# Staging buffers of the weight conversion: pairs and w_out tiles in turn, spare columns and a third buffer

## The chip, the cores and the metric

The kernel runs on one core of a Trainium2 chip. The metric is the device time of one execution in microseconds; three runs of the kernel before took 836.95, 836.95 and 829.41 us. TensorE is called PE in the rows, ScalarE is ACT, VectorE is DVE, SyncE is SP, GpSimd is POOL.

## The reference

Attention with a local or strided mask over 4 batches, 8 heads, 576 positions and 64 dimensions gives x (2304 tokens x 512). Two feed-forward layers follow:

```python
def _moe_ref(x, w_in, w_out, s, b):      # 512 -> 2048 -> 512
    h = x @ w_in
    r = np.maximum(h, 0.0)
    g = s * (r * r) + b
    return (g @ w_out).astype(np.float32)

def _moe2_ref(x, w_in, w_out):           # the same shapes
    h = x @ w_in
    g = h * np.cos(h)
    return (g @ w_out).astype(np.float32)
```

All inputs are float32, and so is the result.

## The kernel before, in words

Every float32 operand of a matmul is split into a high and a low half of a shorter kind, and a product is three matmuls: high x high, high x low, low x high. The weights arrive as 64-bit words (the host only views the float arrays so) and must be turned into float32 and split on the chip, on ScalarE and VectorE; this is the conversion that the change touches.

**Stages.** First the attention runs, with the first slots of layer one between its steps. A slot (40 of them, index t) is one 128-wide part of the hidden layer for a block of tokens: four groups of matmuls into `h_ps`, the activation, and later four groups into `acc` (line 942). The slots cover eight of the sixteen hidden parts of layer one for all tokens. The other eight, and all of layer two's first product, go through units (loop over `u`): a unit is one pair of hidden parts for one region of 768 tokens, seven products of six matmuls each (line 1996, Strassen-like, on sums and differences of operands), with the activation behind it. Units 0 to 11 belong to layer one (three regions, pairs 4 to 7, the order turned in the middle region), units 12 to 19 to layer two's first region. The second product of each unit comes two units later as "triples": eight per unit of layer one (line 1886, each three matmuls of 512 and three of 256 columns), twelve of 512 columns per unit of layer two (line 1876). Two products' PSUM banks alternate; ScalarE evacuates P1, P6 and P7 into `q` (line 2008), VectorE adds the other banks to it and writes `h` (line 1976), ScalarE starts the activation on `h` (line 1433), `gh` and `gl` are its halves. After unit 19 the rest of layer two runs in blocks, with an order written out by hand.

**The conversion jobs.** `jobs2` lists jobs: for each pair of layer one's last four and of layer two's eight, first two pair jobs (`pair_ops`, m = 0, 1: a piece of w_in, converted into `ta`, four sums in `ts`, then halves in the tiles `ob` and `oa`), then two w_out jobs (`out_ops`: one tile, converted into `tw`, or for layer two's even tiles into the spare columns of the `q0` tile, `rq`, and then split into `ow`). The halves are stored to DRAM (`wfa`, `wfb`, `wfc`, `w2s`; for layer two the converted tile itself too, `w2f`) and loaded again as operands (`wfl`, line 1279; `w2l`, line 1312) when a buffer comes free. At the end come six jobs for sums of w_out tiles. Once layer two begins (`late` is set, unit 12), the halves go to other places.

`ob`, `oa` and `ow` are all tiles of one pool tag, `v`, with two buffers that alternate in the order of allocation; an allocation waits until the stores from the tile that it replaces have landed. A job is a generator; each step yields one instruction or an empty step. After attention a pair job has 4 + 4 + 6 + 3 = 17 steps (two of the first four empty), a w_out job 4 + 5 = 9 (two of the first four empty, one later, and for layer one the place of the `w2f` store as well). The load for the job after next is issued in the middle of a job.

**What sets the order.** `bg2_step(n)` adds n to a budget and issues one step for each whole unit of it. It is called eight times per slot from slot 15 on with a rate of `BG2`, and in a unit once after each of the seven products and after each triple (fifteen places in a unit of layer one) with the rate `BG2_UNIT[u]`. All is then placed by a scheduler in each engine's own queue; an instruction may be put ahead of others that were written before it when it is thought to be ready. `tc.issue_after(ins)` orders what is issued within it behind `ins` on the engine of `ins`; it adds no instruction. Before, only the first step of a job is put behind the last relu. SP's queue issues nearly all DMAs in order: raw loads, stores and the loads `wfl` and `w2l`.

The buffers of `w2l` are six tiles with the tags w10 to w15. `BUFS` and `w2_load` say which tile goes where and in which order; a buffer whose last triple is done takes its next tile at once (`load_w2`). Buffer w13 holds layer one's tile of pair 4 until the triples of unit 8, which are issued in unit 10, and then layer two's second tile, needed by the triples of unit 12, which are issued in unit 14.

Of the kernel before, what the change touches and what calls it, by code (L numbers as in the profile page):

```python
# [107 lines left out]
]  # L108
LAST_USE = {"P2": 0, "P5": 1, "P3": 2, "P4": 3}
UNIT0 = ["P1", "P2", "t", "P6", "P5", "P7", "P3", "P4"]  # L110
UNIT = ["P1", "P2", "P6", "P5", "P7", "t", "P3", "P4"]
BG2 = ((15, 1.2), (18, 2.2), (22, 1.0), (30, 1.6), (36, 0.6), (38, 1.2))
BG2_UNIT = (1.2, 2.0, 2.0, 1.4, 1.4, 1.5, 1.5, 1.4, 1.6, 1.7, 1.7, 1.7, 1.4, 1.4, 1.4, 1.4, 1.4, 1.4, 1.4, 1.4, 1.6, 1.6)
NSUM = 6
# [17 lines left out]
def net(ctx, tc, qkl, qks, rqk, vloc, vstr, rv, wi1, wo1, wp1, wo2, wp2, s, b, out):  # L132
# [56 lines left out]
    def to_f32(t, raw):  # L189
        tu = t.bitcast(U32)  # L190
        if raw.shifted:
            top = top_halves()
            t16, mid = raw.halves, raw.middles
            if len(t.shape) == 3:
                top, t16, mid = (x.rearrange("p (i c) -> p i c", i=t.shape[1]) for x in (top, t16, mid))
            out16 = consts.bitcast(F16)[:, 1::2]
            if len(t.shape) == 3:
                out16 = out16.rearrange("p (i c) -> p i c", i=t.shape[1])
            return [
                lambda: nc.scalar.activation(out16, t16, AF.Copy, scale=0.5),  # L200
                lambda: nc.vector.scalar_tensor_tensor(
                    tu, mid, 13, top.bitcast(U32), ALU.logical_shift_right, ALU.bitwise_or
                ),
                lambda: None,
                lambda: None,
            ]
# [176 lines left out]

    late = {}

    def begin_layer2():
# [19 lines left out]
    def pair_ops(raw, ly, p, m):  # L406

        ta = conv_tile("ta").rearrange("p (i c) -> p i c", i=4)
        yield from to_f32(ta, raw)
# [4 lines left out]
        for d, x, y, op in ((s1, a21, a22, ALU.add), (s2, s1, a11, ALU.subtract), (s3, a11, a21, ALU.subtract), (s4, a12, s2, ALU.subtract)):  # L414
            yield lambda d=d, x=x, y=y, op=op: nc.vector.tensor_tensor(d, x, y, op)
        apart = bool(late)
        if apart:
            obs = late_out(0)
# [18 lines left out]
        if apart:  # L437
# [3 lines left out]
            for h in range(2):  # L441
# [4 lines left out]

                yield store
        else:
            yield lambda: nc.sync.dma_start(out=wb[:, :, m, :], in_=ob.bitcast(F32).rearrange("p x h c -> p x (h c)"))
            yield lambda: nc.sync.dma_start(out=wa[:, m, :], in_=oa.bitcast(F32)[:, :512])  # L450
            yield lambda: nc.sync.dma_start(out=wc[:, m, :], in_=oa.bitcast(F32)[:, 512:])
        stored2.add(("pair", ly, p, m))

    def out_load(ly, n):
        return Raw(raw_tile("oraw"), wo_raw[ly][n])

    def out_ops(raw, ly, n):
        t = whole = q0_tile()[:, HT:] if ly and n % 2 == 0 else conv_tile("tw")
        yield from to_f32(t, raw)
        bg2_load()  # L460
        if late:
            os = late_out(n % 2)
            t = t.rearrange("p (x c) -> p x c", x=2)
        else:
            o = io_p.tile([P, 2, 512], F32R, tag="v", name="ow")
            os = [o[:, h, :] for h in range(2)]
        apart = bool(late)
        k = raw.scale
        assert raw.shifted or not ly
        yield lambda: split_hi(os[0], t, k)  # L470
        yield lambda: nc.sync.dma_start(out=w2f[n // 2][:, n % 2, :], in_=whole) if ly else None
# [17 lines left out]
    def sum_ops(raw, p):  # L489

        assert late
        c = raw.rearrange("p (f c) -> p f c", f=2)
        t13, t24 = (conv_tile(x).rearrange("p (x c) -> p x c", x=2) for x in ("t13", "t24"))
# [3 lines left out]
        bg2_load()  # L497
        pair = [(t13, late_out(0)), (t24, late_out(1))]
        for t, o in pair:
            yield lambda t=t, o=o: split_hi(o[0], t, 256.0)  # L500
        for t, o in pair:
            yield lambda t=t, o=o: split_lo(o[1], t, o[0], 256.0)
        for x, (_, o) in enumerate(pair):
# [6 lines left out]

            yield store
        stored2.add(("sum", p))

    jobs2 = []
# [18 lines left out]
    def bg2_load():  # L533
        if jobs2 and len(loaded2) < (1 if gp else 2):
            load, ops, args = jobs2.pop(0)
            loaded2.append(ops(load(*args), *args))

    def bg2_step(n):
        due2[0] += n
        while due2[0] >= 1:  # L540
            due2[0] -= 1
            if now2[0] is None:
# [397 lines left out]

    def mm(*args, **kw):
        nc.tensor.matmul(*args, **kw)  # L942

# [317 lines left out]

    def have(key):
        while key not in stored2:
            bg2_step(1)

    wft, w2t = {}, {}
# [15 lines left out]
    BUFS = [2, 3, 4, 5, 0, 1]  # L1282
    NSTAY = 2
    w2_load = {b_: [] for b_ in BUFS}
    w2_key, w2_last = {}, {}
# [572 lines left out]
    def triple():  # L1858
# [11 lines left out]
        gh, gl = g2[key]  # L1870
        w = w2t[n]
        start = opens[a] and f == 0
        stop = closes[a] and f == 1
# [74 lines left out]
    for u in range(NU2 + 2):  # L1948
# [29 lines left out]
        for what in UNIT0 if u == 0 else UNIT:  # L1978
            if what == "t":
                if u == NU1:  # L1980
                    fetch(2)
                triples(u)
                continue
            x, fi, j, bi, st = PRODUCTS[what]
            while (ly, s_, j) not in formed:
                bg2_step(1)
                tick()
# [4 lines left out]
            fo, lo = P * fi, 256 if x < 3 else P  # L1992
            for m in range(2):
                wh, wl = w[:, m, fo : fo + P], w[:, m, lo + fo : lo + fo + P]
# [135 lines left out]
```

## Time and profile before

| what | value |
|---|---|
| three runs | 836.95, 836.95, 829.41 us; median 836.95 |
| profiled execution | 829.91 us, span 828.1 us |
| TensorE busy | 815.9 us (99%) |
| weight loads busy | 732.4 us (88%) |
| VectorE busy | 629.4 us (76%) |
| ScalarE busy | 586.5 us (71%) |
| granted TensorE clock, mean | 1.000 |

The span runs from the first to the last instruction. Busy time is the union of an engine's instructions; weight loads overlap matmuls. In stretches of the span, the attention and the first slots lie before 145 us, the conversions beside slots until 271, layer one's units until about 480, layer two's first region until 600, the blocks after it.

### The profile page before, as it was taken

The page shows a single profiled execution, that of the slowest core. Times are in us where ns is not written, and L with a number is a line of the kernel's source. Part 1 is how long each engine was busy: PE and PEld are TensorE (multiplying, and loading weights), DVE is VectorE, ACT ScalarE, POOL GpSimd, SP SyncE. Part 2 cuts the span into 40 slices and gives each one's busy share as a digit, 9 for nine tenths or more (in the row PEclk, how much of TensorE's full clock was granted, in tenths as well). Part 3 has the DMA queues.
Part 4 walks back from the last instruction along what each step waited for, and adds up shares of the span by engine and source line. Part 5 has one row for each costly group of instructions (what it writes and reads, how often), then busy time and mean ns, then how long its engine had stood idle before and what let it go on. Part 6 is the DMA issues. An engine that isn't in the chain of part 4 may idle for free.

```text
span 828.1 us, 15377 instructions
## 1 busy us (share of the span) xinstructions
PE 815.9 (99%) x5545; PEld 732.4 (88%) x5545; DVE 629.4 (76%) x1183; ACT 586.5 (71%) x1232; POOL 20.1 (2%) x74
## 2 busy tenths in 40 slices
PE   8899999999999999999989999999999999999998
PEld 5677888788988898999989999888899999999998
DVE  6898555776868769965856598777758999578985
ACT  6897667668876887777768567557568765589753
POOL 3120000000000000000000000000000000000000
PEclk9999999999999999999999999999999999999999
DMA  9775232376889998796799989899797878874675
GB/s 334 240 249 165 82 104 97 127 261 225 325 318 365 359 351 271 284 366 215 283 334 338 305 286 365 297 315 383 257 350 262 273 252 258 286 254 153 207 250 179
DMA packets 101980, 219.98 MB, mean 266 GB/s; under 512 B 9104, under 2 KB 53392, under 8 KB 101904
## 3 DMA queue, kind: packets, MB, share of 16 engines
q1 hardware_dynamic: 100176, 211.82, 74.3%
q10 hardware_dynamic: 1728, 7.18, 2.3%
q8 instruction: 44, 0.72, 0.3%
q14 instruction: 32, 0.26, 0.1%
HBM read 163.91 MB, written 55.05 MB: 264 GB/s over the span
## 4 chain that ended last, share of the span: by engine, by line
PE 76%; ACT 8%; DVE 7%; DMA 7%; issue 1%; POOL 0%; SPq 0%; ACTq 0%; POOLq 0%; DVEq 0%
PE acc L942 10%; PE h_ps L942 10%; PE acc L1876 8%; PE pa L1996 8%; PE acc L1695 8%; PE pb L1996 8%; PE acc L1886 7%; PE acc L1565 6%; PE pa L1565 3%; PE pb L1565 3%; ACT part L684 2%; DVE graw L1157 2%; DVE xlo L171 2%; DMA wfc<-oa 2%; DMA w2s<-ow 2%; DMA wfb<-ob 1%
## 5 line engine op out<-in xcount | busy, mean ns | idle before, releaser
L942 PE MATMUL h_ps<-xhi,w 128*128 128x512 f32 (+1 forms) x320 | 102.4, 378 | 0.6 <-ACT xhi L166 0.5
L942 PE MATMUL acc<-gh,w 128*128 128x512 f32 (+1 forms) x320 | 101.5, 375 | 0.1
L1886 PE MATMUL acc<-gh,w2l 128*128 128x512 f32 (+1 forms) x384 | 85.2, 336 | 0.0
L1996 PE MATMUL pb<-xhi,wfl 128*128 128x384 f32 x268 | 80.5, 340 | 1.7 <-DVE h L1976 1.6
L1996 PE MATMUL pa<-xhi,wfl 128*128 128x384 f32 x268 | 79.7, 338 | 0.7 <-ACT q L2008 0.7
L166 ACT ACTIVATE xhi<-graw 128x384 fp32r<-128x384 f32 (+1 forms) x84 | 51.2, 629 | 38.4 <-DVE graw L1157 18.3
L942 PEld LDWEIGHTS h_ps<-xhi,w 128*128 128x128 f32 x320 | 58.5, 189 | 11.9 <-ACT xhi L166 0.9
L942 PEld LDWEIGHTS acc<-gh,w 128*128 128x128 f32 x320 | 58.6, 189 | 11.1 <-ACT gh L166 0.5
L1695 PE MATMUL acc<-xhi,w2m 128*128 128x384 f32 x256 | 67.1, 335 | 0.0
L1886 PEld LDWEIGHTS acc<-gh,w2l 128*128 128x128 f32 x384 | 59.9, 188 | 7.4 <-DMA w2l<-w2s 0.2
L171 DVE TENSOR_TENSOR xlo<-graw,xhi 128x384 fp32r<-128x384 f32 (+1 forms) x84 | 55.0, 688 | 7.5 <-ACT xhi L166 7.5
L1876 PE MATMUL acc<-w2l,gh 128*128 128x512 f32 x192 | 60.0, 390 | 0.0
L942 PE MATMUL acc<-gl,w 128*128 128x512 f32 (+1 forms) x160 | 59.4, 371 | 0.0
L942 PE MATMUL h_ps<-xlo,w 128*128 128x512 f32 (+1 forms) x160 | 59.3, 371 | 0.0
L1433 ACT ACTIVATE h<-h 128x768 f32<-128x768 f32 x48 | 40.3, 839 | 23.6 <-DVE h L1976 23.5
L1565 PE MATMUL acc<-xhi,wfl 128*128 128x384 f32 x196 | 55.3, 335 | 0.1
L1996 PEld LDWEIGHTS pb<-xhi,wfl 128*128 128x128 f32 x268 | 49.4, 188 | 5.4 <-DVE h L1976 3.3
L171 DVE TENSOR_TENSOR gl<-r,gh 128x512 fp32r<-128x512 f32 (+2 forms) x56 | 40.7, 726 | 15.9 <-ACT gh L1433 8.3
L1996 PEld LDWEIGHTS pa<-xhi,wfl 128*128 128x128 f32 x268 | 49.4, 188 | 2.9 <-ACT q L2008 1.6
L1886 PE MATMUL acc<-gl,w2l 128*128 128x512 f32 x192 | 49.1, 336 | 0.0
L1695 PEld LDWEIGHTS acc<-xhi,w2m 128*128 128x128 f32 x256 | 46.5, 188 | 0.0
L1996 PE MATMUL pb<-xlo,wfl 128*128 128x384 f32 x134 | 45.0, 336 | 0.0
(249 smaller groups left out, 2075.7 us busy)
## 6 DMA issues: line engine op xcount, KB each, us to landing
wfl<-wfb SPq DMA_DIRECT2D x68, 512.0 KB, 5.2
wfl<-wfa SPq DMA_DIRECT2D x34, 512.0 KB, 5.5
w2l<-w2s SPq DMA_DIRECT2D x28, 512.0 KB, 5.4
w2m<-wsum SPq DMA_DIRECT2D x22, 512.0 KB, 3.9
wfb<-ob SPq DMA_DIRECT2D x21, 512.0 KB, 4.5
w2s<-ow SPq DMA_DIRECT2D x20, 512.0 KB, 5.5
praw<-in_wp_dram SPq DMA_DIRECT2D x20, 511.8 KB, 6.0
oraw<-in_wo_dram SPq DMA_DIRECT2D x20, 511.8 KB, 5.5
```

The lines of the kernel that those rows point to most:

```text
L166: nc.scalar.activation(dst_hi, src, AF.Copy, scale=scale)
L171: return nc.vector.tensor_tensor(dst_lo, src, hi.bitcast(F32), ALU.subtract)
L684: nc.scalar.activation(self.p[j][:, t, :], src[:, t, :], AF.Exp, bias=self.sm[j][:, 0, t : t + 1], scale=SCALE if self.pe_mask else 1.0, a ...
L942: nc.tensor.matmul(*args, **kw)
L1157: return nc.vector.tensor_tensor(d, x, y, op)
L1433: return nc.scalar.activation(*args, **kw)
L1565: nc.tensor.matmul(self.bank(v, bi), a, b[:, m, :], start=st and m == 0 and i == 0, stop=m == 1 and i == 2, skip_group_check=True)
L1695: nc.tensor.matmul(self.acc(j, e), w[u][:, wi, c], g[:, u], start=first and i == 0, stop=last and i == 2, skip_group_check=True)
L1876: nc.tensor.matmul(accs[e], g[:, e * P : (e + 1) * P], w[:, wi, :], start=start and i == 0, stop=stop and i == 2, skip_group_check=True,)
L1886: nc.tensor.matmul(o, w[:, wi, e * P : (e + 1) * P], g[:, c : c + o.shape[1]], start=start and i == 0 and (c == 0 or e % 2 == 0), stop=sto ...
L1996: nc.tensor.matmul(pb[bi], a, b[:, m, :], start=st and m == 0 and i == 0, stop=m == 1 and i == 2, skip_group_check=True)
```

## The change

- `jobs2` takes a pair job, a w_out job, a pair job, a w_out job for each pair.
- The empty steps after the conversion and in `out_ops` go (a pair job has 15 steps, a w_out job 6), and the rates are lowered.
- Layer one's w_out tiles: the high half goes to the spare columns of the `q0` tile, the low half is written in place over the converted tile; two stores of one half each instead of one store.
- Layer two's w_out tiles before `late`: as before in a tile of `v`, but in buffer w13 once its last tile of layer one is used up. Its load of layer two's tile is put off to unit 12.
- Every step is issued behind `front[0]`, the last relu of a slot or the last evacuation `q` of a unit.
- `sent` and `landed` keep a modelled time at which a place's stores have landed, in columns of matmul traced so far; a step that finds it ahead yields WAIT and the job is put off. `LANDS` is 0.

```diff
+LANDS = 0
+DUE = 6
+WAIT = object()
-BG2 = ((15, 1.2), (18, 2.2), (22, 1.0), (30, 1.6), (36, 0.6), (38, 1.2))
-BG2_UNIT = (1.2, 2.0, 2.0, 1.4, 1.4, 1.5, 1.5, 1.4, 1.6, 1.7, 1.7, 1.7, 1.4, 1.4, 1.4, 1.4, 1.4, 1.4, 1.4, 1.4, 1.6, 1.6)
+BG2 = ((15, 1.0), (18, 2.0), (22, 0.9), (30, 1.3), (36, 0.5), (38, 1.0))
+BG2_UNIT = (1.0, 1.5, 1.5, 1.3, 1.3, 1.3, 1.3, 1.3, 1.3, 1.3, 1.3, 1.3, 1.2, 1.2, 1.2, 1.2, 1.2, 1.2, 1.2, 1.3, 1.4, 1.4)
...
     def out_ops(raw, ly, n):
+        yield from landed((ly, n), "spare") if ly and n % 2 == 0 else landed((ly, n))
         t = whole = q0_tile()[:, HT:] if ly and n % 2 == 0 else conv_tile("tw")
         yield from to_f32(t, raw)
         bg2_load()
-        if late:
+        apart = bool(late)
+        place_ = ("out", n % 2) if apart else third_place[0] if ly and third_place else stage_v() if ly else "spare"
+        yield from landed(place_)
...
+        if apart:
             os = late_out(n % 2)
             t = t.rearrange("p (x c) -> p x c", x=2)
-        else:
-            o = io_p.tile([P, 2, 512], F32R, tag="v", name="ow")
+        elif ly:
+            o = wp.tile([P, 2, 512], F32R, tag=place_, name="ow", bufs=1) if place_ in third_place else io_p.tile([P, 2, 512], F32R, tag="v", name="ow")
             os = [o[:, h, :] for h in range(2)]
+        else:
+            os = [x.bitcast(F32R) for x in (q0_tile()[:, HT:], t)]
         yield lambda: split_hi(os[0], t, k)
...
         yield lambda: split_lo(os[1], t, os[0], k)
-        yield lambda: None
...
+        elif ly:
+            yield lambda: nc.sync.dma_start(out=w2s[ly, n], in_=o.bitcast(F32))
         else:
-            yield lambda: nc.sync.dma_start(out=w2s[ly, n], in_=o.bitcast(F32))
+            for h in range(2):
+                yield lambda h=h: nc.sync.dma_start(out=w2s[ly, n][:, h, :], in_=os[h].bitcast(F32))
...
+    def columns(n):
+        traced[0] += n / 2400
+
+    def sent(*places):
+        for x in places:
+            landing[x] = traced[0] + LANDS
+
+    def landed(*places):
+        while not forced[0] and any(landing.get(x, 0) > traced[0] for x in places):
+            yield WAIT
+
+    def behind():
+        return tc.issue_after(front[0].ins) if front[0] is not None else nullcontext()
...
-        for m in range(2):
-            jobs2.append((pair_load, pair_ops, (ly, p, m)))
-        for f in range(2):
-            jobs2.append((out_load, out_ops, (ly, 2 * p + f)))
+        for i in range(2):
+            jobs2.append((pair_load, pair_ops, (ly, p, i)))
+            jobs2.append((out_load, out_ops, (ly, 2 * p + i)))
...
                 now2[0] = loaded2.pop(0)
-                with tc.issue_after(relu[0].ins):
-                    next(now2[0])()
-                continue
             op = next(now2[0], None)
             if op is None:
                 now2[0] = None
                 due2[0] += 1
+            elif op is WAIT:
+                due2[0] = min(due2[0] + 1, DUE)
+                return
             else:
-                op()
+                with behind():
+                    op()
...
-        relu[0] = nc.scalar.activation(r, h, AF.Relu)
+        front[0] = relu[0] = nc.scalar.activation(r, h, AF.Relu)
...
+        if w2_load[b_] and w2_load[b_][0][0] and b_ == THIRD and not late:
+            third_place.append(f"w1{b_}")
+            return
...
                 if u == NU1:
                     fetch(2)
+                    if third_place:
+                        load_w2(THIRD)
...
-                    evac[u, q] = nc.scalar.activation(qs[q], pb[0], AF.Copy)
+                    front[0] = evac[u, q] = nc.scalar.activation(qs[q], pb[0], AF.Copy)
```

## Rows read from the trace of the kernel before

**Rows 1.** The page, busy us (share of the span) xinstructions by engine.

```profile
PE 815.9 (99%) x5545; PEld 732.4 (88%) x5545; DVE 629.4 (76%) x1183; ACT 586.5 (71%) x1232; POOL 20.1 (2%) x74
```

**Rows 2.** Busy time by stretch of the span; columns as the first line names them.

```profile
core 0: us, PE busy (x) PEld busy (x) DVE busy (x) ACT busy (x) POOL busy (x), PEclk, DMA share, GB/s
0.00:145.00 145.00, 139.41 (x1754) 106.56 (x1755) 103.25 (x273) 112.39 (x437) 19.12 (x71) 1.00 0.55 182
145.00:271.00 126.00, 126.00 (x756) 107.94 (x755) 94.08 (x207) 93.17 (x196) 0.97 (x3) 1.00 0.76 272
271.00:480.00 209.00, 206.05 (x1162) 189.00 (x1161) 152.48 (x279) 153.15 (x243) 0.00 (x0) 1.00 0.87 309
480.00:600.00 120.00, 119.97 (x599) 107.31 (x599) 94.71 (x147) 77.14 (x118) 0.00 (x0) 1.00 0.91 318
```

**Rows 3.** Chain that ended last, in order of time: start us, us, what.

```profile
371.09 8.32 PE acc L1886 x48
...
690.79 16.64 PE acc L1695 x96
```

**Rows 4.** Instructions of tile w2l: duration ns min/median/max, first and last start us.

```profile
L1886 PEld LDWEIGHTS acc<-gh,w2l x384: 186/188/191, 283.2 to 476.0; 128*128 128x128 f32 x192
```

**Rows 5.** Waits of PE, 271 to 480 us: us in total, times, longest us.

```profile
PE pb L1996 <- DVE h L1976: 1.6, 2, 1.4
PE pa L1996 <- ACT q L2008: 1.2, 3, 0.7
```

**Rows 6.** Timeline of ACT, PE and DVE: start us, us, instruction [idle before <-releaser].

```profile
355.67 0.63 ACT L166 ACTIVATE ow<-q 128x512 fp32r<-128x512 f32 x1 [0.23 <-DMA wfb<-ob]
...
357.31 0.62 ACT L166 ACTIVATE ow<-tw 128x512 fp32r<-128x512 f32 x1
...
363.59 0.63 ACT L166 ACTIVATE ob<-ts 128x512 fp32r<-128x512 f32 x1 [2.87 <-DMA w2s<-ow]
...
365.47 0.44 PE L1996 MATMUL pb<-xhi,wfl 128*128 128x384 f32 x1 [0.16 <-DVE h L1976]
...
429.07 0.63 ACT L166 ACTIVATE ow<-tw 128x512 fp32r<-128x512 f32 x1 [4.51 <-DMA wfc<-oa]
...
429.73 0.69 DVE L170 SCALAR_TENSOR_TENSOR ow<-tw,ow 128x512 fp32r<-128x512 f32 x1 [4.18 <-ACT ow L166]
430.34 0.55 DVE L1976 TENSOR_TENSOR h<-pb,q 128x384 f32<-128x384 f32 x1
430.81 0.55 DVE L1976 TENSOR_TENSOR h<-pa,q 128x384 f32<-128x384 f32 x1
...
430.95 0.44 PE L1996 MATMUL pb<-xhi,wfl 128*128 128x384 f32 x1 [1.44 <-DVE h L1976]
```

**Rows 7.** Waits of all engines, 411 to 420 us.

```profile
ACT oa L166 <- DMA wfc<-oa: 0.8, 1, 0.8
PE pa L1996 <- ACT q L2008: 0.7, 1, 0.7
```

**Rows 8.** Groups of ACT, 145 to 271 us: busy us, mean ns, idle before, releasers.

```profile
L166 ACT ACTIVATE oa<-ta 128x256 fp32r<-128x256 f32 (+1 forms) x20 | 6.4, 352 | 4.3 <-DMA w2s<-ow 2.2 <-DMA wfc<-oa 2.0
L166 ACT ACTIVATE ob<-ts 128x512 fp32r<-128x512 f32 x10 | 6.3, 629 | 6.0 <-DVE ts L415 4.2 <-DMA wfb<-ob 1.8
```

**Rows 9.** Instructions of tile ow, its stores on SP's queue.

```profile
L481 SPq DMA_DIRECT2D w2s<-ow x20: 319/320/1477, 168.3 to 431.5; - x20
```

**Rows 10.** DMA issues, 271 to 480 us: count, KB each, median us to landing.

```profile
w2l<-w2s SPq DMA_DIRECT2D x13, 512.0 KB, 6.0
...
wfb<-ob SPq DMA_DIRECT2D x11, 512.0 KB, 5.6
```

**Rows 11.** Tile ob, whole span: its stores from issue to landing.

```profile
DMA to landing us min/median/max: 2.7/4.5/9.2
```

**Rows 12.** Waits of SP's queue, 271 to 480 us.

```profile
SPq L1279 <- PE pa L1996: 26.6, 19, 6.0
```

More of the change, by code (lines that the diff above doesn't have):

```diff
@@ L203, in to_f32 @@
                 ),
-                lambda: None,
-                lambda: None,
             ]
@@ L384, in net @@
     late = {}
+    third_place = []
     def begin_layer2():
@@ L406, in pair_ops @@
     def pair_ops(raw, ly, p, m):
+        yield from landed((ly, p, m))
         ta = conv_tile("ta").rearrange("p (i c) -> p i c", i=4)
@@ L416, in pair_ops @@
         apart = bool(late)
+        places = (("out", 0), ("out", 1)) if apart else (stage_v(), stage_v())
+        yield from landed(*places)
+        if late and not apart:
+            apart, places = True, (("out", 0), ("out", 1))
         if apart:
@@ L447, in pair_ops @@
                 yield store
+            sent(*places)
         else:
@@ L451, in pair_ops @@
             yield lambda: nc.sync.dma_start(out=wc[:, m, :], in_=oa.bitcast(F32)[:, 512:])
+            sent(*places)
         stored2.add(("pair", ly, p, m))
@@ L457, in out_ops @@
     def out_ops(raw, ly, n):
+        assert raw.shifted or not ly
+        yield from landed((ly, n), "spare") if ly and n % 2 == 0 else landed((ly, n))
         t = whole = q0_tile()[:, HT:] if ly and n % 2 == 0 else conv_tile("tw")
@@ L460, in out_ops @@
         bg2_load()
-        if late:
+        apart = bool(late)
+        place_ = ("out", n % 2) if apart else third_place[0] if ly and third_place else stage_v() if ly else "spare"
+        yield from landed(place_)
+        if late and not apart:
+            apart, place_ = True, ("out", n % 2)
+        if apart:
             os = late_out(n % 2)
             t = t.rearrange("p (x c) -> p x c", x=2)
-        else:
-            o = io_p.tile([P, 2, 512], F32R, tag="v", name="ow")
-            os = [o[:, h, :] for h in range(2)]
-        apart = bool(late)
+        elif ly:
+            o = wp.tile([P, 2, 512], F32R, tag=place_, name="ow", bufs=1) if place_ in third_place else io_p.tile([P, 2, 512], F32R, tag="v", name="ow")
+            os = [o[:, h, :] for h in range(2)]
+        else:
+            os = [x.bitcast(F32R) for x in (q0_tile()[:, HT:], t)]
         k = raw.scale
-        assert raw.shifted or not ly
         yield lambda: split_hi(os[0], t, k)
-        yield lambda: nc.sync.dma_start(out=w2f[n // 2][:, n % 2, :], in_=whole) if ly else None
+        if ly:
+            yield lambda: nc.sync.dma_start(out=w2f[n // 2][:, n % 2, :], in_=whole)
+            if n % 2 == 0:
+                sent("spare")
         yield lambda: split_lo(os[1], t, os[0], k)
-        yield lambda: None
         if apart:
@@ L479, in out_ops @@
                 )
-        else:
-            yield lambda: nc.sync.dma_start(out=w2s[ly, n], in_=o.bitcast(F32))
+        elif ly:
+            yield lambda: nc.sync.dma_start(out=w2s[ly, n], in_=o.bitcast(F32))
+        else:
+            for h in range(2):
+                yield lambda h=h: nc.sync.dma_start(out=w2s[ly, n][:, h, :], in_=os[h].bitcast(F32))
+        sent(place_)
         stored2.add(("out", ly, n))
@@ L491, in sum_ops @@
         assert late
+        yield from landed((p,))
         c = raw.rearrange("p (f c) -> p f c", f=2)
@@ L498, in sum_ops @@
         pair = [(t13, late_out(0)), (t24, late_out(1))]
+        yield from landed(("out", 0), ("out", 1))
         for t, o in pair:
@@ L511, in sum_ops, with stage_v @@
             yield store
+        sent(("out", 0), ("out", 1))
         stored2.add(("sum", p))
+    traced, forced = [0.0], [False]
+    landing = {}
+    def columns(n):
[6 more added lines that the diff above has]
+            yield WAIT
+    front = [None]
+    def behind():
+        return tc.issue_after(front[0].ins) if front[0] is not None else nullcontext()
+    turn_v = [0]
+    def stage_v():
+        turn_v[0] += 1
+        return "v", turn_v[0] % 2
     jobs2 = []
     for ly, p in [(0, p) for p in range(PAIR1, NPAIR)] + [(1, p) for p in range(NPAIR)]:
-        for m in range(2):
-            jobs2.append((pair_load, pair_ops, (ly, p, m)))
-        for f in range(2):
-            jobs2.append((out_load, out_ops, (ly, 2 * p + f)))
+        for i in range(2):
+            jobs2.append((pair_load, pair_ops, (ly, p, i)))
+            jobs2.append((out_load, out_ops, (ly, 2 * p + i)))
     jobs2 += [(sum_load, sum_ops, (p,)) for p in range(NSUM)]
@@ L535, in bg2_load @@
             load, ops, args = jobs2.pop(0)
+            sent(args)
             loaded2.append(ops(load(*args), *args))
@@ L939, in h_bank, with mm @@
         return psum("h" if t % 2 == 0 else "att", "h_ps")
-    def mm(*args, **kw):
-        nc.tensor.matmul(*args, **kw)
+    def mm(o, *args, **kw):
+        columns(o.shape[1])
+        nc.tensor.matmul(o, *args, **kw)
     def mm_h(t, c):
@@ L1262, in have @@
     def have(key):
+        forced[0] = True
         while key not in stored2:
             bg2_step(1)
+        forced[0] = False
     wft, w2t = {}, {}
@@ L1283, in net @@
     NSTAY = 2
+    THIRD = 3
     w2_load = {b_: [] for b_ in BUFS}
@@ L1871, in triple @@
         w = w2t[n]
+        columns(3 * (512 if ly else SBT))
         start = opens[a] and f == 0
@@ L1985, in net @@
             while (ly, s_, j) not in formed:
+                forced[0] = True
                 bg2_step(1)
+                forced[0] = False
                 tick()
@@ L1992, in net @@
             fo, lo = P * fi, 256 if x < 3 else P
+            columns(6 * HT)
             for m in range(2):
```

## The prediction

> **What bounds the kernel now.** I read the busy totals of the page first [rows 1]. TensorE is busy for 815.9 of 828.1 us, ScalarE for 586.5. A change that moves only conversions and their buffers removes no matmul, so what it can give back is TensorE's idle time. The table by stretch [rows 2] shows where that lies: from 145 to 271 us, where layer one's pairs and w_out tiles are converted beside the slots, TensorE is busy for 126.00 of 126 us; from 271 to 480 us, in the twelve units of layer one, for 206.05 of 209; from 480 to 600 us for 119.97 of 120. The conversions have ended before 600. The granted clock is 1.00 (2.4 GHz) in all these stretches, so no change of level is at stake. The whole prize is therefore 209 - 206.05 = 2.95 us in the third stretch and 0.03 us in the fourth.
>
> That a busy TensorE here means a running one I check by pace [rows 3]: 96 matmuls of 384 columns take 16.64 us, 173 ns each, and the 48 matmuls of one unit's triples (half with 512 columns, half with 256) take 8.32 us, 173 ns on average too, with no gap inside either. A unit has 42 matmuls of 384 columns as well, so it lasts 42 x 0.1733 + 8.32 = 15.6 us; twelve make 187 us, which with the tail of the slots fits the stretch.
>
> One rule would see more room. In the third stretch weight loads are busy for 189.00 of 209 us [rows 2], which leaves 20 us, where the matmul column leaves 2.95. The Trainium skill (Trainium Kernel Development and Optimization, Performance Expectations) says that matmul busy time is a bad metric of the distance to the roofline, and that the busy share of weight loads is a good one; by it up to 20 us could be had in this stretch. The rows speak against using it so: one load takes 188 ns [rows 4] beside a matmul that takes over 188 ns where it has 512 columns, so loads have gaps wherever 512 columns stream, without TensorE ever stopping. I go by 2.95.
>
> **What the 2.95 us are made of.** The waits of TensorE in this stretch are 1.6 us on the sums that DVE adds into h and 1.2 us on ScalarE's evacuations q [rows 5]. Followed back, the large ones begin at a staging buffer. At 429.07 us the high half of a w_out tile (ow) has waited 4.51 us on ScalarE for the store of oa; DVE's low half comes 0.66 us behind it at 429.73, the two sums h behind that, and TensorE resumes at 430.95 after 1.44 us [rows 6]. At 363.59 us ob has waited 2.87 us for the store of an ow tile, and TensorE lost 0.16 us [rows 6]. Around 418 us a wait of 0.8 us for the store of oa stands beside a TensorE wait of 0.7 us on q [rows 7]. So TensorE has some 2.7 us of cover for a ScalarE wait at a staging buffer: between the two priced waits it pays (1.44 - 0.16) / (4.51 - 2.87) = 0.78 us for each further us. The rest of the 2.95 us is not tied to these buffers.
>
> **Part by part.** *Layer one's w_out halves out of the staging pair.* Eight tiles are converted with their high half in the spare columns and the low half in place, so only pairs use the two v buffers there. The waits that this removes are 1.8 us at ob and 2.2 + 2.0 us at oa on ScalarE [rows 8], all in the stretch where TensorE never stops: worth 0. What hides them now is ScalarE's slack, 93 of 126 us busy [rows 2]. Each tile's store becomes two; eight more DMA issues at about 0.32 us [rows 9] are 2.6 us on SP's queue, which holds nothing that TensorE waits for then: 0. If that cover were gone, 2.6 us would be the whole price.
>
> *Fewer steps at lower rates.* The empty steps fall away: 34 + 18 steps for two pairs and two w_out tiles become 30 + 12. The rates fall too. Counting from the rates in the diff, steps per slot and unit give 268.8 by the first unit and 542.5 by the thirteenth before; 232 and 457.5 after. In tiles that is (542.5 - 208) / 52 = 6.4 groups of layer two by the thirteenth unit before and (457.5 - 168) / 42 = 6.9 after. Conversions finish a little earlier, none has to be forced: 0.
>
> *Pairs and w_out in turn, for layer two.* This is where the order can hurt. The two v buffers alternate. Before, with pair, pair, w_out, w_out, the tightest reuse is the first w_out tile, seven steps after the store of the ob that it replaces; at 1.4 to 1.7 steps in each of fifteen places of a 15.6 us unit that is 5.2 to 4.3 us. After, each w_out tile takes the buffer of the pair just ahead of it, five steps after that store; at 1.3 steps it is 5 x 0.80 = 4.0 us. The store wfb<-ob lands in 5.6 us in the median of this stretch [rows 10], 9.2 us at most anywhere [rows 11]. So a typical w_out tile now waits 1.6 us on ScalarE, below the 2.7 us of cover, and costs nothing; the worst waits 5.2 us and costs (5.2 - 2.7) x 0.78 = 2.0 us. About ten tiles of layer two (five groups) come before the third buffer. Bounds: 0, and ten waits like the longest seen, 10 x 1.44 = 14.4 us. I take one bad one in the ten, near the middle of its size: +1.0 us.
>
> *Every ScalarE conversion behind the last evacuation.* Before, only the first operation of a job is ordered behind a relu; the rest run ahead. It shows: the high halves of two successive w_out tiles stand at 355.67 and 357.31 us, and the next pair's ob already asks for its buffer after 360.72 [rows 6], where the steps written between them, nine and then thirteen, would be some 6 and 9 us. That bunching is what made ob wait 2.87 us. Ordering edges add no instruction. They take such waits away; of the 1.44 + 0.70 + 0.16 = 2.30 us that rows tie to staging I take half, -1.2 us, since the closer reuse above acts against it. Bounds: 0 and -2.95. What is queued behind a waiting ScalarE conversion is the next evacuation q and, through the low half on DVE, the sums h.
>
> *The third buffer.* It is free only once the unit with index 8 has had its triples, in the unit with index 10; by then 6.3 groups of layer two are converted, by the thirteenth unit 6.9, so it carries one or two w_out tiles: -0.1 us at most. Its weight load is issued two units later, in the thirteenth, and is needed two units on, 31 us, against 6.0 us to landing [rows 10]: 0. SP's queue is already held up to 6.0 us at a time by weight loads that wait for TensorE [rows 12], so this load may land later than 6.0; the cover of 31 us would have to go five times over.
>
> *The modelled landings* do nothing: with LANDS = 0 a place's landing time never lies ahead of the traced time, so no job is put off.
>
> **The sum.** 829.91 us (the profiled execution; its span is 828.1 and 1.8 lie around it) - 1.2 - 0.1 + 1.0 = 829.6, say 829.5 us: no change to be seen. That execution stands with the fastest of the three runs (829.41); the median, 836.95, is 7.5 us above it, more than twice all the idle time that this trace has in the stretches changed, so nothing here says where those runs lost it.
>
> **Rivals.** (B) *The staging waits go entirely.* Against it: the reuse distances above; for it: the bunched order is plain. At most 829.91 - 2.95 = 827.0 us, 0.35% under the profiled execution, though 1.2% under the median. (C) *Staging waits move into layer two's w_out tiles.* ScalarE waits for wfb<-ob at each of ten tiles, and q and h stand behind it. For it: five steps against a landing of 5.6 us; against it: the cover of 2.7 us. If all ten cost what the one at 429 us cost: 829.91 + 14.4 - 1.2 = 843 us; from six such waits on (8.6 us) it is over 1%. The Trainium skill (TensorE: Matmul & The Clock Gate, Architectural detail) has ScalarE's queue strictly first-in first-out; by that rule nothing behind such a tile can pass it, and the order at 429 us agrees. (D) *The headroom of 20 us that the weight loads leave is real*, and a better order of the queues yields it: 829.91 - 20 = 810 us. The page on the metric is the rule meant above; the pace of the matmuls speaks against it. (E) *The change doesn't do what it says*: no landing is ever waited for and the third buffer comes too late to matter, so the order alone is different and the time stays where before's upper runs lie, 837 us.
>
> **How the numbers follow.** Within 1% is what a measurement of this kernel can tell from no change. Forecast 0.55: 829.5 us, within 1% of either end of before's runs but for a tail of 0.05 that falls over 1% under their median. B 0.25: 827 us, 0.17 of it faster by over 1%, since it needs the median of before to stay high. C 0.13: 0.11 slower. D 0.02, faster. E 0.05, same. Faster 0.05 + 0.17 + 0.02 = 0.24; slower 0.11; within 0.65. The range runs from 824, which is B's 827.0 less 0.3% of scatter, to 840, which is the upper runs with the same scatter and a fifth of C; it leaves out D, most of C and the edges.
>
> **What would show it.** Right: TensorE idles 2 to 4 us in the units of layer one, with no longer list of waits than before; ScalarE waits 1 to 2 us at many w_out tiles for the store of ob; oa and ob wait nowhere before 271 us; high halves of successive tiles stand 5 us or more apart. Wrong: waits of ScalarE over 4 us at several w_out tiles, each followed by TensorE waiting on h or q (C); no wait at all and TensorE busy for the whole stretch (B); TensorE idle in the thirteenth to fifteenth unit for the late weight load, whose cover I took for granted; or a loss in the first 145 us, which the change doesn't touch.

## The result, and the profile after

The change makes the kernel half a per cent slower: 836.43 us in the median (832.61 to 844.46, 22 runs) against 832.23 (827.53 to 837.37, 22 runs on the same chip), ratio 1.0056 [1.0038, 1.0075]. The profiled execution took 839.10 us with a span of 837.3. The page's busy totals, which answer to [rows 1]:

```profile
PE 818.0 (98%) x5545; PEld 735.4 (88%) x5545; DVE 628.4 (75%) x1181; ACT 584.9 (70%) x1232; POOL 19.9 (2%) x74
```

The matmuls are as many and take 2.1 us longer; of the 9.2 us between the two spans the other 7.1 are idle time of TensorE. The two profiled executions lie further apart than the medians do (9.2 against 4.2 us), so not all of this belongs to the change. The table by stretch of after shows where, against [rows 2]:

```profile
core 0: us, PE busy (x) PEld busy (x) DVE busy (x) ACT busy (x) POOL busy (x), PEclk, DMA share, GB/s
0.00:145.00 145.00, 137.65 (x1743) 105.96 (x1744) 101.48 (x267) 110.02 (x427) 18.75 (x70) 0.99 0.56 179
145.00:271.00 126.00, 124.94 (x748) 106.54 (x747) 94.76 (x212) 94.45 (x208) 1.19 (x4) 1.00 0.77 273
271.00:480.00 209.00, 203.03 (x1137) 186.80 (x1136) 148.50 (x276) 151.58 (x241) 0.00 (x0) 0.99 0.88 308
480.00:600.00 120.00, 118.79 (x600) 106.47 (x599) 93.96 (x143) 73.49 (x111) 0.00 (x0) 1.00 0.92 310
```

TensorE's idle time grows from 5.59 to 7.35 us before 145 us, where the change has moved nothing yet (the first conversions start after 144 us, and ScalarE and VectorE run the same instructions in the same order up to 140 us in both traces: scatter of one execution), from 0 to 1.06 up to 271, from 2.95 to 5.97 up to 480, and from 0.03 to 1.21 up to 600. TensorE's waits of after from 271 to 480 us, beside [rows 5] (us in total, times, longest us):

```profile
PE pb L2060 <- DVE h L2035: 3.8, 2, 2.9
PE pb L2060 <- ACT q L2072: 1.2, 1, 1.2
PE pa L2060 <- ACT q L2072: 1.0, 1, 1.0
```

Four waits: two on q at the passage from the slots to the units, one of 0.91 us on a sum h that ends at 308.35, not followed further here, and one near 430 us. First the passage. Its timeline in after (start us, us, instruction, idle before and releaser), beside [rows 6]:

```profile
276.37 0.63 ACT L169 ACTIVATE ow<-q 128x512 fp32r<-128x512 f32 x1 [1.18 <-DMA wfb<-ob]
276.90 0.83 ACT L169 ACTIVATE xdiff<-xt 128x768 fp32r<-128x768 f32 x1
277.64 0.47 ACT L2072 ACTIVATE q<-pa 128x384 f32<-128x384 f32 x1
...
278.16 0.44 PE L2060 MATMUL pa<-xdiff,wfl 128*128 128x384 f32 x1 [0.99 <-ACT q L2072]
...
283.74 0.62 ACT L169 ACTIVATE ob<-ts 128x512 fp32r<-128x512 f32 x1
284.26 1.01 ACT L1502 ACTIVATE h<-h,sb 128x768 f32<-128x768 f32 x1
285.17 0.47 ACT L2072 ACTIVATE q<-pb 128x384 f32<-128x384 f32 x1
...
285.69 0.62 PE L2060 MATMUL pb<-xdiff,wfl 128*128 128x384 f32 x2 [1.20 <-ACT q L2072]
```

At 276 us ow waits 1.18 us for a store, and TensorE waits 0.99 us for the evacuation q behind it. At 284 us nothing waits for a store at all: a conversion (ob) and the bias step on h stand ahead of q and run back to back, and TensorE loses 1.20 us. That q cannot pass them agrees with the strict first-in first-out queue of the Trainium skill (TensorE: Matmul & The Clock Gate, Architectural detail). In the kernel before, the q of that place stands ahead of both, and TensorE has six matmuls of another group to run meanwhile, so its own order differs there too:

```profile
278.29 0.47 ACT L2008 ACTIVATE q<-pb 128x384 f32<-128x384 f32 x1
278.66 1.02 ACT L1444 ACTIVATE h<-h,sb 128x768 f32<-128x768 f32 x1
...
279.58 0.62 ACT L166 ACTIVATE ob<-ts 128x512 fp32r<-128x512 f32 x1
```

The second place, near 430 us:

```profile
427.73 0.63 ACT L169 ACTIVATE ow<-tw 128x512 fp32r<-128x512 f32 x1 [2.38 <-DMA wfb<-ob]
...
436.74 0.61 ACT L169 ACTIVATE oa<-ta 128x256 fp32r<-128x256 f32 x2 [3.35 <-DMA w2s<-ow]
437.19 0.42 DVE L173 SCALAR_TENSOR_TENSOR oa<-ta,oa 128x256 fp32r<-128x256 f32 x1 [2.90 <-ACT oa L169]
437.54 0.55 DVE L2035 TENSOR_TENSOR h<-pb,q 128x384 f32<-128x384 f32 x1
...
438.14 0.44 PE L2060 MATMUL pb<-xhi,wfl 128*128 128x384 f32 x1 [2.87 <-DVE h L2035]
```

A w_out tile waits 2.38 us for the pair's store, its own store goes out that much later and lands 7.6 us after its issue (5.2 in the median of ow's stores), and the next oa waits 3.35 us for that one. Through DVE's low half and the sum h, TensorE loses 2.87 us. The place is not new: 15 of the 20 traces, before's among them with 1.44 us, have a TensorE stall over 0.5 us between 428 and 438 us. The windows after it (columns as in the table by stretch) show a second cost:

```profile
434.90:438.10 3.20, 0.37 (x2) 0.00 (x0) 0.91 (x3) 0.61 (x2) 0.00 (x0) 1.00 1.03 417
...
439.60:443.00 3.40, 3.40 (x13) 3.40 (x12) 1.51 (x2) 2.38 (x4) 0.00 (x0) 0.50 0.75 243
443.00:446.40 3.40, 3.40 (x21) 3.24 (x20) 1.42 (x4) 3.24 (x6) 0.00 (x0) 1.00 0.65 189
```

The granted clock is 0.50 (1.2 GHz) from 439.6 to 443.0 us, 13 matmuls where the next equal stretch has 21: half of 3.4 us, 1.7 us, on top of the 2.87. This trace has one more such stretch, from 33.4 to 36.8 us, in the attention, which the change doesn't touch; the trace of before has none. Over the timed runs, (1 - mean granted clock) x time is 2.5 us in after's 22 and 0.9 to 1.6 in the five sets of before's runs that stand beside the experiments, so an estimate of 0.9 to 1.6 of the 4.2 us between the medians is clock.

ScalarE's groups from 145 to 271 us in after, the counterpart of [rows 8]:

```profile
L169 ACT ACTIVATE oa<-ta 128x256 fp32r<-128x256 f32 (+1 forms) x22 | 7.1, 353 | 0.4 <-DMA w2s<-ow 0.4
L169 ACT ACTIVATE ob<-ts 128x512 fp32r<-128x512 f32 x11 | 6.9, 628 | 5.2 <-DVE ts L418 5.2
```

The waits of ob for a store are gone there and those of oa are down to 0.4 us, as forecast. But the longest wait for a store at a staging buffer in the whole trace has come into the same stretch, at a w_out tile of layer two right behind its pair:

```profile
259.12 0.63 ACT L169 ACTIVATE ow<-tw 128x512 fp32r<-128x512 f32 x1 [5.50 <-DMA wfb<-ob]
```

ScalarE stands for 5.50 us, so its store waits there are 5.9 us in all, where before has 6.0. TensorE runs on through it; it stops at 267.9 us, for 1.06 us, and whether that follows from this wait is not shown. The stores themselves land as late as before, by after's DMA issues from 271 to 480 us, beside [rows 10]:

```profile
wfb<-ob SPq DMA_DIRECT2D x11, 512.0 KB, 5.7
```

### The profile page after: what moved, and what is told of

The parts are those of the page before. It is cut to its first block, busy times and chain, and to the rows that moved or that the text cites. A ratio compares the mean times of both kernels' runs of the same rounds, so it can differ in the third digit from the quotient of the medians.

```text
span 837.3 us, 15384 instructions
## 1 busy us (share of the span) xinstructions
PE 818.0 (98%) x5545; PEld 735.4 (88%) x5545; DVE 628.4 (75%) x1181; ACT 584.9 (70%) x1232; POOL 19.9 (2%) x74
```

## Experiments

All ratios are against the kernel before on the same chip. The table has what the sections use: ratio and median, TensorE's idle us in four stretches of the one profile of each kernel, and ScalarE's waits for stores at staging buffers from 271 to 480 us.

| kernel | ratio [95%] | us | 260-320 | 320-420 | 420-480 | 480-620 | store waits |
|---|---|---|---|---|---|---|---|
| before | | | 0.54 | 0.87 | 1.54 | 0.03 | 9.0 |
| after | 1.0056 [1.0038, 1.0075] | 836.43 | 4.16 | 0.00 | 2.87 | 1.21 | 8.7 |
| e1_lands5 | 1.0008 [0.9982, 1.0033] | 832.71 | 1.28 | 1.26 | 2.28 | 0.00 | 6.9 |
| e2_order_back | 1.0042 [1.0015, 1.0070] | 834.81 | 4.22 | 1.14 | 1.80 | 0.21 | 12.2 |
| e3_edges_back | 1.0045 [1.0026, 1.0065] | 835.48 | 2.05 | 0.56 | 2.45 | 0.22 | 9.2 |
| e4_no_third | 1.0059 [1.0038, 1.0079] | 836.43 | 5.82 | 0.00 | 2.00 | 0.41 | 10.5 |
| e5_turn_alone | 1.0021 [0.9997, 1.0045] | 833.92 | 1.30 | 1.12 | 0.25 | 1.56 | 17.3 |
| e6_edges_alone | 0.9979 [0.9963, 0.9996] | 829.35 | 0.34 | 0.00 | 0.62 | 1.14 | 3.1 |
| e7_steps_back | 1.0000 [0.9984, 1.0017] | 831.03 | 2.19 | 0.00 | 1.11 | 0.72 | 7.1 |
| e8_lands_stage | 1.0029 [1.0008, 1.0050] | 833.89 | 1.68 | 2.77 | 2.03 | 0.00 | 11.4 |
| e9_space_out | 1.0017 [0.9994, 1.0040] | 832.99 | 2.64 | 0.01 | 1.74 | 1.33 | 6.6 |
| e10_space_pair | 1.0010 [0.9992, 1.0027] | 833.20 | 2.14 | 0.60 | 0.26 | 2.18 | 7.8 |
| e11_steps_order_back | 1.0015 [0.9996, 1.0033] | 832.65 | 3.18 | 0.00 | 0.35 | 1.44 | 1.9 |
| e12_old_spread | 1.0021 [1.0001, 1.0041] | 833.47 | 0.00 | 0.07 | 3.22 | 2.63 | 9.0 |
| e13_early_back | 1.0034 [1.0010, 1.0058] | 834.69 | 1.88 | 0.63 | 2.20 | 0.79 | 9.2 |
| e14_late_back | 1.0085 [1.0057, 1.0114] | 839.27 | 3.80 | 1.16 | 3.46 | 0.01 | 10.2 |
| e15_edges_spare | 1.0075 [1.0048, 1.0101] | 837.40 | 1.80 | 1.26 | 1.78 | 5.24 | 9.7 |
| e16_no_spare | 1.0072 [1.0045, 1.0100] | 838.41 | 3.66 | 1.83 | 0.00 | 1.93 | 5.9 |
| e17_passage_free | 1.0072 [1.0048, 1.0096] | 837.43 | 2.13 | 0.00 | 2.68 | 3.11 | 9.4 |
| e18_edges_again | 0.9970 [0.9949, 0.9991] | 830.21 | 0.58 | 0.00 | 0.07 | 1.17 | 2.0 |

**The parts undone one by one.** e1 (landings modelled at 5 us), e2 (order), e3 (edges on a job's first step only), e4 (third buffer never used), each from after:

```
e1 -LANDS = 0
   +LANDS = 5
e2 -        for i in range(2):
   -            pair (ly, p, i), then out (ly, 2 * p + i)
   +        for m in range(2): pair (ly, p, m)
   +        for f in range(2): out (ly, 2 * p + f)
e3 -                with behind():
   +                with behind() if first_[0] else nullcontext():   # behind the last relu
e4 -        if ... and b_ == THIRD and not late:
   +        if ... and b_ == -1 and not late:
```

> The changed kernel with LANDS = 5: a job is put off until 5 us of matmuls have been traced since the stores from its place. Staging theory (a w_out tile of layer two stands right behind its pair and its halves wait on ScalarE for the pair's store; q and h stand behind it): the waits of ow, ob and oa for stores fall from 7 us between 271 and 480 us to under 2, no TensorE wait over 1 us is left in layer one's units, no half clock after 400 us, ratio to the kernel before 0.998 to 1.002. Edge theory (every conversion behind the last evacuation makes q and h late): the edges are all still there, so the ratio stays 1.004 to 1.007. Buffer theory (the third buffer and its late load cost the time): also 1.004 to 1.007.

> The changed kernel with the old order of jobs (pair, pair, w_out, w_out), all else as changed. Staging theory: the reuse distance of a w_out tile behind its pair is met once per group instead of twice, so about half the loss goes: ratio 1.000 to 1.004, ScalarE's waits at ow, ob and oa about half. Edge theory: 1.004 to 1.007. Buffer theory: 1.004 to 1.007.

> The changed kernel with only the first step of a job ordered, behind the last relu, as before. Staging theory: the tight reuse stays and jobs bunch again, so the ratio stays 1.004 to 1.010 with waits of ScalarE at ow and oa of 5 us or more in total. Edge theory: back to 0.998 to 1.002. Buffer theory: 1.004 to 1.007.

> The changed kernel without the third buffer: layer two's w_out tiles stay in v and the weight load of w13 comes in unit 10 again. Staging theory: one or two more w_out tiles can wait, ratio 1.004 to 1.009. Buffer theory: back to 0.998 to 1.002. Edge theory: 1.004 to 1.007.

Undoing the order, the edges or the third buffer leaves the loss at 0.42 to 0.59%, so none of them alone is its cause; e4's 1.0059 beside 1.0056 puts the third buffer at nothing. e1 takes the loss to 1.0008, with steps and rates as in after; why, its profile doesn't settle, since it has 6.9 us of store waits, not under 2 as expected, and after 8.7, and three TensorE waits over 1 us are left.

**Two parts put alone into before.** e5 has the order in turn (e2's edit the other way round), e6 the edges:

```
e6 -                with tc.issue_after(relu[0].ins):      # a job's first step
   +                with tc.issue_after(front[0].ins):     # and every other step
   +        front[0] = relu[0] = nc.scalar.activation(r, h, AF.Relu)
   +        front[0] = evac[u, q] = nc.scalar.activation(qs[q], pb[0], AF.Copy)
```

> The kernel before with only the order of jobs changed (pair, w_out, pair, w_out); empty steps, rates, edges and buffers as before. Order theory (a w_out tile right behind its pair reuses that pair's buffer too early): at least half of the loss, ratio 1.002 to 1.006. Step theory (it is the two empty steps that are gone between conversion and halves which bring the reuse too close): 0.998 to 1.002. Edge theory: 0.998 to 1.002.

> The kernel before with only the edges: every step of a job is ordered behind the last relu or evacuation. Edge theory: ratio 1.002 to 1.006. Order theory and step theory: 0.996 to 1.002, since pacing takes the bunching away.

The order alone is worth +0.21% with 1 inside the interval, though ScalarE's store waits nearly double to 17.3 us. The edges alone gain 0.21%. Neither is the +0.56%. Nor do they carry over: undone from after, the order gives back 0.14 points, and the edges, a gain alone, 0.11 (e2, e3), neither resolved by the intervals.

**The steps and the rates.** e7 gives after the empty steps and the rates of before; e8 takes e1's landings without the raw loads':

```
e7 +                lambda: None,     # twice in to_f32
   +        yield lambda: None        # in out_ops
   -BG2 = ((15, 1.0), (18, 2.0), ...   BG2_UNIT = (1.0, 1.5, 1.5, 1.3, 1.3, ...
   +BG2 = ((15, 1.2), (18, 2.2), ...   BG2_UNIT = (1.2, 2.0, 2.0, 1.4, 1.4, ...
e8  e1, and in bg2_load:
   -            sent(args)
```

> The changed kernel with the empty steps put back (two after a conversion, one in a w_out job) and the old rates; order, spare columns, third buffer and edges as changed. Step theory: back to 0.998 to 1.002, stalls of TensorE from 260 to 610 us about 5 us as in the kernel before. Order theory: 1.003 to 1.007. Edge theory: 1.004 to 1.007.

> The changed kernel with LANDS = 5 for the staging places alone; a job no longer waits for the modelled landing of its raw load. Staging theory: like e1, ratio 0.998 to 1.003. Raw-load theory (what e1 took away were waits of conversions for raw loads at the head of ScalarE's queue): 1.004 to 1.007.

e7 is level with before, 1.0000 [0.9984, 1.0017], with order, edges, spare columns and third buffer all in place: in after, putting back the steps and rates that I had costed at nothing removes the whole loss. e8, with landings modelled for the staging places alone, gives back about half (1.0029), with 11.4 us of store waits; it doesn't decide between its two theories. The windows of e7 (columns as in the table by stretch):

```profile
260.00:290.00 30.00, 27.81 (x150) 25.08 (x149) 22.69 (x44) 20.42 (x36) 0.00 (x0) 1.00 0.95 362
290.00:320.00 30.00, 30.00 (x171) 27.67 (x171) 19.71 (x41) 22.42 (x37) 0.00 (x0) 1.00 0.93 321
320.00:420.00 100.00, 100.00 (x574) 92.89 (x573) 81.83 (x148) 76.39 (x121) 0.00 (x0) 1.00 0.79 275
420.00:480.00 60.00, 58.89 (x338) 54.61 (x337) 38.76 (x71) 40.26 (x63) 0.00 (x0) 1.00 0.99 349
```

And the same windows of after:

```profile
260.00:290.00 30.00, 26.75 (x144) 23.72 (x143) 22.70 (x45) 20.70 (x39) 0.00 (x0) 1.00 0.96 343
290.00:320.00 30.00, 29.09 (x164) 26.54 (x164) 20.00 (x41) 24.93 (x40) 0.00 (x0) 1.00 0.89 314
320.00:420.00 100.00, 100.00 (x571) 92.19 (x570) 81.86 (x150) 72.65 (x115) 0.00 (x0) 1.00 0.82 288
420.00:480.00 60.00, 57.13 (x320) 53.15 (x319) 34.30 (x64) 42.44 (x68) 0.00 (x0) 0.97 0.93 326
```

ScalarE does less from 260 to 320 us in e7 (42.84 against 45.63 us) and from 420 to 480 (40.26 against 42.44), more between, where there is room; TensorE idles 3.3 us from 260 to 480 in place of 7.0, and keeps its clock. How much ScalarE does is not all of it, though: before has 45.60 us of ScalarE from 260 to 320 and idles 0.54. Which evacuation the conversions stand ahead of must count too; that is argued from the timelines above, not shown by a run.

**Which of the two, and where.** From after: e9 has empty steps in the w_out jobs alone, e10 in the pair jobs alone, each with rates raised in proportion; e12 has no empty steps and before's rates scaled to the shorter jobs; e13 has steps and rates of before up to the fourth unit only, e14 from the fifth on only. e11 is e7 with the old order.

```
e9  +  two empty steps after to_f32 and one after split_lo in out_ops; rates x 48/42
e10 +  two empty steps after to_f32 in pair_ops; rates x 46/42
e11 e7, and e2's loops
e12 +BG2 = ((15, 0.969), (18, 1.777), (22, 0.808), (30, 1.292), (36, 0.485), (38, 0.969))
    +BG2_UNIT = (0.969, 1.615, 1.615, 1.131, ...      # old x 42/52, later x 50/60
e13 empty steps where unit_now[0] < 4, old rates there
e14 empty steps where unit_now[0] >= 4, old rates there
```

> The changed kernel with the empty steps put back in w_out jobs alone (two after the conversion, one before the store) and the new rates times 48/42, so that as many tiles are converted per unit. A w_out tile then reuses the pair's buffer seven steps after its store, not five. Step theory, reuse by ow decides: waits of ow for wfb from 9 to under 5 us, ratio 0.999 to 1.003. Step theory, reuse by oa decides: 1.003 to 1.006. Rate theory (how the conversions are spread over slots and units decides): 1.004 to 1.007.

> The changed kernel with two empty steps put back after the conversion in pair jobs alone and the new rates times 46/42. The second pair's oa then reuses the first w_out tile's buffer ten steps after its store, not eight, and the high half of ob comes two steps later behind its sums. Step theory, reuse by ow decides: 1.003 to 1.007. Step theory, reuse by oa decides: 0.999 to 1.003. Rate theory: 1.004 to 1.007.

> The changed kernel, without empty steps, with the old rates times 42/52 up to unit 11 and 50/60 from unit 12: the conversions are spread over slots and units as in the kernel before, but the steps stay close together. Step theory: 1.004 to 1.007. Rate theory: 0.998 to 1.002.

> The changed kernel with empty steps, rates and the order of jobs as before; what is left of the change is the edges, the spare columns for layer one and the third buffer. Step theory and order theory: 0.996 to 1.000, as the edges alone. Buffer theory: 1.000 to 1.004. A version that may beat both kernels.

> The changed kernel with empty steps and rates as before in the slots and up to unit 3, and as changed from unit 4 on. Passage theory (the loss arises where the units begin, 260 to 320 us, as conversions stand ahead of evacuations and sums): ratio 0.999 to 1.003, TensorE idle from 260 to 320 us under 2.5 us. Reuse theory (it arises at layer two's w_out tiles later): 1.003 to 1.006.

> The changed kernel with empty steps and rates as before from unit 4 on, and as changed ahead of it. Passage theory: 1.003 to 1.006, TensorE idle from 260 to 320 us 4 us or more as in the changed kernel. Reuse theory: 0.999 to 1.003.

e9, e10 and e12 each give back over half of the 0.56%, by different means, and their intervals overlap: rates and empty steps are not told apart. e13 gives back 0.22 points, e14 comes out higher (1.0085, its interval overlapping after's), while both together (e7) give back all: the halves don't add up. By place, e13's idle time from 260 to 320 us falls to 1.88 us and e14's stays at 3.80, as the passage theory had it; in e12, with the conversions spread as before, it is 0.00. The store waits don't order the kernels: e11 has 1.9 us of them at 1.0015, e18 2.0 at 0.9970, e5 17.3 at 1.0021, e16 5.9 at 1.0072.

**The spare columns, the passage, and the edges again.** e15 is e6 with layer one's w_out halves in the spare columns and in place; e16 is after without that; e17 is after with no conversions in the last slots and the first two units; e18 is e6 once more.

```
e15 e6, and for layer one:
   +            os = [x.bitcast(F32R) for x in (q0_tile()[:, HT:], t)]
   +            two stores, one for each half
e16 -  that branch of out_ops, and its two stores
e17 +BG2 = ((15, 1.0), (18, 2.0), (22, 0.9), (30, 1.6), (36, 0.0), (38, 0.0))
    +BG2_UNIT = (0.0, 0.0) + (1.45,) * 10 + ...
```

> The kernel before with the edges and layer one's w_out halves in the spare columns and in place; order, steps, rates and buffers as before. If the spare columns cost something: 1.000 to 1.003. If they cost nothing, as the prediction has it: 0.996 to 1.000, as the edges alone (e6).

> The changed kernel with layer one's w_out halves in a tile of v and one store, as before. If the spare columns cost something: 1.001 to 1.004. If they cost nothing: 1.004 to 1.008, the further waits for v lying ahead of 271 us, where TensorE doesn't stop.

> The changed kernel with no conversion steps in slots 36 to 39 and in units 0 and 1, a rate of 1.6 in slots 30 to 35 and 1.45 in units 2 to 11. Passage theory: TensorE idle from 260 to 320 us under 1.5 us, ratio 1.000 to 1.003, what is left being the wait near 430 us and its half clock. Rival (the passage is slow for another reason, such as the spills that DMA carries there): TensorE idle from 260 to 320 us 3 us or more, ratio 1.004 to 1.007.

> The kernel before with only the edges, once more. If the gain is one of the edges: ratio 0.996 to 0.999. If it was the chip of e6: 0.999 to 1.003.

e17 tests the reading of the passage. Its TensorE waits from 260 to 480 us are two groups only:

```profile
PE pb L2060 <- DVE h L2035: 2.6, 1, 2.6
PE pa L2060 <- DVE h L2035: 2.1, 2, 1.2
```

The waits on q near 277 and 285 us are gone, with the conversions that stood ahead of q; conversions begin again at 282 us, and the losses come at 301 (0.90) and 317 (1.23), on sums h. So the two stalls on q come with the conversions. But idle time from 260 to 320 us is 2.13 us, between the two expectations, and the ratio 1.0072: with the passage freed the loss is still there, elsewhere, among others in 3.11 us of waiting for a weight load at 607 us. In e15 that wait is longer still, 5.24 us from 609.7 (e6, to which e15 adds the spare columns, has 1.14), for a weight load that stands on SP's queue behind stores of the sums:

```profile
PE acc L1572 <- DMA wfl<-wfb: 5.2, 1, 5.2
```

The spare columns' own price stays open. Put into e6 they lose 0.96 points (e15), taken out of after they give nothing back (e16), and e11, which is e15 with the third buffer and one step less in each of layer one's eight w_out jobs, is at 1.0015. Those steps put e15's conversions some 5 us later (an ob at 288 us that e11 has at 283), so e15's loss may be pacing as well; no run separates the two. It also shows that a loss of this size comes without after's steps and rates. e18 repeats e6's gain, on a chip of the same number, so that another chip would show it is not tested. Its windows:

```profile
260.00:320.00 60.00, 59.42 (x331) 54.56 (x331) 46.01 (x92) 46.00 (x77) 0.00 (x0) 1.00 0.92 348
320.00:420.00 100.00, 100.00 (x574) 92.65 (x573) 80.38 (x147) 75.24 (x120) 0.00 (x0) 1.00 0.84 289
420.00:480.00 60.00, 59.93 (x341) 55.02 (x341) 39.19 (x68) 41.15 (x64) 0.00 (x0) 1.00 0.98 349
```

Before with the edges alone beats both kernels, by 0.2 to 0.3% against before.

## Why the prediction was right and wrong

The forecast was no change, at 829.5 us beside a profiled 829.91. Within 1% it is no change, and 836.43 lies in the range; but a loss of 0.56% is resolved, and the forecast did not have it. That 836.43 lies in the range is luck: the range went up to 840 for the upper runs of before and a part of rival C, not for a loss of this kind. Of the 6.9 us between forecast and measurement 4.2 are the change; 2.3 are the base, since 829.91 was a good execution of a kernel whose median over 22 runs is 832.23, and the rest is the forecast gain.

- **Failed: "Fewer steps at lower rates: 0".** I counted groups converted by the thirteenth unit and saw that none was forced. By e7, undoing this part is worth 0.56%, 4.7 us: when the conversions run, and beside what, has a price though all of them finish in time. e7, which has the rest, is at 1.0000, where the sum without this part would have put it; since the parts don't add elsewhere, that agreement is partly luck. How the price is split between rates and empty steps is not shown, nor what the part costs alone, put into before. e1 removes the loss without touching it and e15 has a loss without it; so a rival stands that every edit places the conversions anew, and the time follows from the few evacuations that they meet, whichever part moves them.
- **Failed with it: "some 2.7 us of cover".** I took it from two waits in the middle of the units. At the passage a wait of 1.18 us cost 0.99, and a conversion that waited for nothing cost 1.20: a conversion's own time counts, not only its wait. Near 430 us two waits in a row, 2.38 and 3.35 us, used the cover up; and 5.50 us at 259 us, beside the slots, stopped nothing at once. So the cover is no one number. The second wait near 430 us, oa behind the w_out tile's store, was a reuse that my sum left out, since I counted the steps behind ob's store alone.
- **Edges, "-1.2 us": right, and more, put alone into before:** -0.21 and -0.30%, 1.7 to 2.5 us. Within after, undoing them changes the ratio by 0.11 points, which the intervals don't resolve (e3). e18's store waits fall to 2.0 us from 9.0.
- **Order in turn, "+1.0": right within the interval**, 0.21%, 1.7 us, with bounds of -0.3 and +4.5 per mille, which hold 0 as well.
- **Third buffer and modelled landings: right.** Without the buffer e4 is 0.03 points slower, far inside the intervals. With LANDS = 0 nothing is put off; the landings do something once they are 5 us (e1).
- **Spare columns, 0:** right where I looked, since the waits of ob and oa before 271 us went and freed nothing. The 5.50 us of ow at 259 us are the order in turn, which I priced in the units alone; TensorE's 1.06 us behind it are a wait on DVE. The spare columns' own price is open.
- **Rivals.** C (waits at ten w_out tiles) came true in small: after has three waits for ob's store at ow, 5.50, 1.18 and 2.38 us, where before has two of 0.5 us together and one of 4.51 for oa's; from 271 to 480 us all store waits are 8.7 us against 9.0. Its mechanism, q and h queued behind ScalarE, holds at 276 and 430 us; its size, ten such waits, doesn't. B fell. D fell: the Trainium skill (Trainium Kernel Development and Optimization, Performance Expectations) would have the weight loads' busy share as the metric of the room left; in e18 from 420 to 480 us they are busy for 55.02 of 60 us while TensorE idles 0.07, so the other 5 us are no stop that a better order of the queues could take away. E's 837 us are near what came, but its reason, an order that changes nothing, is not what the runs show.
- **Not foreseen: the clock.** "No change of level is at stake" held for before, but not where a stall is new.

What stays open: the split between rates and empty steps, whether they cost anything outside this kernel's other changes, and the spare columns; each kernel has one profile, so a stall seen in one of them is a place, not a price.

## What to carry to other kernels

Where an engine with a strict queue does both helper work and evacuations, the schedule of the helper steps is part of the critical path even when its total is hidden: price each step by what stands behind it, at the stage with the least cover, not by whether the whole finishes in time. Ordering every helper step behind the last evacuation paid here (0.9979 and 0.9970); putting back the placeholders and rates that looked free to change gave back 0.56% of the changed kernel. Before adding up parts, measure one alone and one undone: here they did not add.

## What the runs showed of the hardware

After an idle stretch of TensorE the granted clock fell to 0.50 for some 3.4 us and the matmuls in it took twice as long: in after at 439.6 us behind 2.87 us of waiting, in e2 at 289.2 behind 1.83, in e11 at 274.7 behind 1.98, each worth about 1.7 us (an estimate from the halved clock). It did not always: e12 idled 3.14 us from 429.0 and e1 2.28 from 430.9, and both kept 1.00. A stall of two or three microseconds is thus to be priced with up to 1.7 us more.
